# Weight conversion at the start of a fused FFT and MLP kernel: the clamps of fifteen weight blocks and six subtractions move from VectorE to GpSimd

## The chip, the cores and the metric

The kernel runs on one core of one Trainium2 chip. The metric is the device time of one execution in microseconds. Of the kernel before, three executions took 903.04, 904.01 and 903.05 us: a median of 903.05 us. The engines are named as the profile names them: PE (TensorE, the matmuls), DVE (VectorE), ACT (ScalarE), POOL (GpSimd) and SP (the queue that issues most DMAs).

## What is computed

A two-dimensional Fourier transform whose real part goes through an MLP with a gated activation:

```python
def _attn_ref(x):                       # x: 4 x 3008 x 256, float32
    X = np.fft.fft(x, axis=1)
    X = np.fft.fft(X, axis=2)
    return X.real.astype(np.float32)

def _moe_ref(x, w_in, w_out):           # 12032 x 256, 256 x 2048, 2048 x 256
    h = x @ w_in
    g = h * (1.0 / (1.0 + np.exp(-h)))
    return (g @ w_out).astype(np.float32)
```

`w_in` and `w_out` are float64. The chip has no such type here: the kernel reads each weight as two 32-bit words and builds the float32 out of their bits.

## The kernel before

The sequence transform is split into classes of output columns: 4 batches x 4 classes = 16 chunks `c` of 376 or 378 columns. The transform along the 256 features is folded into the weights: each of eight blocks of `w_in` (256 columns each) is multiplied by a DFT matrix (`project`, L523), and the products are kept in a high and a low part, `abh` and `abl` (`large` L532, `small` L536). A chunk then goes through 16 steps `f`, each of 128 hidden columns: `first` (L396 to L402) multiplies the chunk by `abh` and `abl` into the PSUM tile `pq` (two buffers), `act` (L414 to L431) adds and subtracts on DVE into `h` and takes the Silu on ACT into `g`, and `second` (L456 to L465), three steps behind, multiplies by `w_out` into four accumulators. In chunk 0 the first twelve steps use the whole float32 `w_out` block `wo_f32` (tile `wof`, L456); later steps use a high part `woh` and a low part `wol` (L458, L459, L465).

The order of instructions on each engine is the order in which this Python code emits them, and no scheduler changes it. Each engine runs its own list in order; semaphores tie the lists together. So an instruction that waits holds back all that stand behind it on its engine.

**The conversion of a block** is the generator `to_f32` (L70 to L85): an Abs on ACT (L77) of the upper word read as a float32, a clamp on DVE (L79), a double shift on DVE (L81), and two combined steps on DVE that bring in the lower word and the sign (L83, L85). Eight blocks of `w_in` (tile `wf`, raw tile `win`, four buffers) are converted between 4 and 40 us, each followed by `project`. In `ahead` (L512) a block's Abs is emitted; `convert` runs the rest. Eight blocks of `w_out` (raw tile `wo`, three buffers in two tags, so that block q + 3 is loaded when block q has been converted) follow from `convert_all_wo` (L124), a generator that yields between steps. The main loop draws on it: four `next` calls in step 0 of chunk 0, and in `act` two or three more per step (the argument `fill`), which places the steps between the additions of `h` on DVE. Blocks 0 to 5 become `wo_f32`; blocks 6 and 7 are split at once. Of blocks 0 to 5, `split_wo` (L116) makes the parts later: a copy to `woh` on ACT (L119) and a subtraction to `wol` on DVE (L121); these six lie between 71 and 108 us.

**GpSimd** issues some DMAs and does small arithmetic. In the first 110 us its list holds, in order: three fills, an accumulating DMA into the tile `raw` (`add_x`, L158) that waits for that tile's load, eight small DMAs of a row of the projected weights (L529) and one broadcast (`ub`, L377), five fills (L682, L288 to L290), a second `add_x` of 1 MB, three DMAs of the transform tables `te`, `to` and `t2` (L539, 1.1 MB each), and the subtractions `xl` of chunk 1's operand (L320). Ahead of its first arithmetic instruction the program has a row `ISA`, which loads the code that GpSimd needs for such arithmetic; fills and DMAs need none.

Of the kernel before, what the change touches and what calls it, by code (L numbers as in the profile page):

```python
# [24 lines left out]
F32 = mybir.dt.float32  # L25
# [4 lines left out]
ALU = mybir.AluOpType  # L30
# [15 lines left out]
W_MIN = float(np.uint32(896 << 20).view(np.float32))  # L46
W_MAX = float(np.uint32((1151 << 20) - 1).view(np.float32))
# [3 lines left out]
def fft_mlp(ctx, tc, x1, x2, w_in, w_out, te, to, t2, t2f, rot1, rot2, dft, eye, out):  # L51
    nc = tc.nc
    ctx.enter_context(tc.manual_schedule())
    tt = nc.vector.tensor_tensor
# [12 lines left out]
    zero = wts.tile([1, 256], F32, name="zero")  # L67
    turn = wts.tile([128, 1], F32, name="turn")
    vneg = fold_p.tile([128, 2, CH], F32R, tag="ri1", name="vneg")
    def to_f32(raw, dst):  # L70

        words = [raw.bitcast(d).rearrange("p c (n t) -> p c n t", t=2) for d in (U32, F32)]
        lo, hi, hf = words[0][:, :, :, 0], words[0][:, :, :, 1], words[1][:, :, :, 1]
        t = dst.bitcast(U32)
        nc.scalar.activation(dst, hf, AF.Abs)  # L77
        yield
        nc.vector.tensor_scalar(dst, dst, W_MIN, W_MAX, op0=ALU.max, op1=ALU.min)  # L79
        yield  # L80
        nc.vector.tensor_scalar(t, t, 5, 2, op0=ALU.logical_shift_left, op1=ALU.logical_shift_right)  # L81
        yield
        stt(t, lo, 29, t, op0=ALU.logical_shift_right, op1=ALU.bitwise_or)  # L83
        yield
        stt(t, hi, 0xC0000000, t, op0=ALU.bitwise_and, op1=ALU.bitwise_or)  # L85
# [13 lines left out]
    def load_wo(q, queue=nc.sync):  # L99

        tag = "od" if q % 3 == 2 else "ri0"
        wo_raw[q] = fold_p.tile([128, 2, D], I64, tag=tag, name="wo", bufs=1 + (tag == "ri0"))
        queue.dma_start(out=wo_raw[q], in_=w_out[q * 256:(q + 1) * 256, :].rearrange("(f p) d -> p f d", p=128))

    def convert_wo(q):
        if q < FULL // 2:
            yield from to_f32(wo_raw.pop(q), wo_f32[q])
            return
        wf = fold_p.tile([128, 2, D], F32, tag="half", name="wf", bufs=3)
        yield from to_f32(wo_raw.pop(q), wf)  # L110
        wh, wl = wo[0][q], wo[1][q]
        nc.scalar.activation(wh, wf, AF.Copy)
        yield
        tt(wl, wf, wh.bitcast(F32), op=ALU.subtract)

    def split_wo(q):  # L116
        wf, wh = wo_f32[q], wo[0][q]
        wl = wo[1][q] = wts.tile([128, 2, D], F32R, tag="wof", name="wol", bufs=FULL // 2 + 1)
        nc.scalar.activation(wh, wf, AF.Copy)  # L119
        yield 0.7  # L120
        tt(wl, wf, wh.bitcast(F32), op=ALU.subtract)  # L121
        yield 0.6

    def convert_all_wo():  # L124

        work = convert_wo(0)
        next(work)
        for q in range(NF // 2):
            for _ in range(2):
                next(work)  # L130
                yield
            if q + 1 < NF // 2:
                following = convert_wo(q + 1)
                next(following)
            yield from work
            if q + 3 < NF // 2:
                load_wo(q + 3)
            work = following
            yield
# [5 lines left out]
    def pq_tile():  # L145
        return pq_p.tile([128, 2, 512], F32, tag="pq", name="pq")
# [241 lines left out]
    def first(c, f):  # L388
        uvh, uvl, _, n, _ = chunks[c]
        fs = slice(f * 128, (f + 1) * 128)  # L390
        pq = pqs[c, f] = pq_tile()
        if c == 0 and f < DIRECT:
            for i, (vh, vl) in enumerate(((uvh[:, 1], uvl[:, 1]), (vneg[:, 0], vneg[:, 1]))):
                for m, (oh, ol) in enumerate(((uvh[:, 0], uvl[:, 0]), (vh, vl))):
                    for p, (a, x) in enumerate(((abh, oh), (abh, ol), (abl, oh))):
                        nc.tensor.matmul(pq[:, i, :n], a[:, m, fs], x[:, :n], start=m + p == 0, stop=m + p == 3)  # L396
            return
        for i in range(2):
            po = pq[:, i, :n]
            nc.tensor.matmul(po, abh[:, i, fs], uvh[:, i, :n], start=True, stop=False)  # L400
            nc.tensor.matmul(po, abh[:, i, fs], uvl[:, i, :n], start=False, stop=False)  # L401
            nc.tensor.matmul(po, abl[:, i, fs], uvh[:, i, :n], start=False, stop=True)  # L402
    def signs(c, f):

        return (slice(0, 1), slice(1, 2)) if c == 4 * B - 1 and f >= NF - 2 else (slice(0, 2),)

    def act(c, f, fill=()):
        pq, (_, _, ub, n, _) = pqs.pop((c, f)), chunks[c]
        direct = c == 0 and f < DIRECT
        if not direct:  # L410
            h = mp.tile([128, 2, CH], F32, tag="h", name="h", bufs=3)
            p = h[:, 1]
        if not direct:
            stt(p[:, :n], ub[:, :n], a128[f // 2][:, f % 2:f % 2 + 1], pq[:, 0, :n], op0=ALU.mult, op1=ALU.add)  # L414
        for work in fill[:1]:
            next(work, None)
        if not direct:
            tt(h[:, 0, :n], p[:, :n], pq[:, 1, :n], op=ALU.add)  # L418
            tt(h[:, 1, :n], p[:, :n], pq[:, 1, :n], op=ALU.subtract)  # L419
        for work in fill[1:]:  # L420
            next(work, None)
        if c == 0 and f < FULL:
            g = gp.tile([128, 2, CH], F32, tag=("gh", "gl")[f % 2], name="g")
            nc.scalar.activation(g[:, :, :n], (pq if direct else h)[:, :, :n], AF.Silu)
            gs[c, f] = g
            return
        gh = gp.tile([128, 2, CH], F32R, tag="gh", name="gh")
        gl = gp.tile([128, 2, CH], F32R, tag="gl", name="gl")
        for sg in signs(c, f):
            nc.scalar.activation(h[:, sg, :n], h[:, sg, :n], AF.Silu)  # L430
            nc.scalar.activation(gh[:, sg, :n], h[:, sg, :n], AF.Copy)  # L431
        gs[c, f] = gh, gl, h
# [73 lines left out]
    win, wf32, pws, conv = {}, {}, {}, {}  # L506
# [4 lines left out]

    def ahead(q):  # L512
        wf32[q] = fold_p.tile([128, 2, 256], F32, tag="half", name="wf", bufs=3)
        conv[q] = to_f32(win.pop(q), wf32[q])
        next(conv[q])

    def project(q):

        w = wf32.pop(q)
        pw = pws[q] = ps.tile([128, 2, 256], F32, tag="ps", name="pw")  # L520
        for m in range(2):
            for c in range(2):
                nc.tensor.matmul(pw[:, m, :256], dft_sb[:, c, m, :], w[:, c], start=c == 0, stop=c == 1)  # L523
# [10 lines left out]
    def small(q):  # L534
        fs = slice(q * 256, (q + 1) * 256)
        tt(abl[:, :, fs], pws.pop(q)[:, :, :256], abh[:, :, fs].bitcast(F32), op=ALU.subtract)  # L536
# [70 lines left out]
    wo_work = convert_all_wo()  # L607
# [28 lines left out]
    for b in range(1, B - 1):  # L636
        c = 4 * b + 1
# [10 lines left out]
    for n in range(len(steps) + LAG):  # L648
        c, f = steps[min(n, len(steps) - 1)]
        if n < len(steps):  # L650
            first(c, f)
        if n == 0:
            project(7)
            for _ in range(4):
                next(wo_work)
            small(6)
        if n >= LAG:
            second(*steps[n - LAG])
        new = None
        if n < len(steps):  # L660
            if f == 12 and c + 1 < 4 * B:
                drain(queue, upto=("op", c + 1))
                drain(pool_queue, upto=("x", c + 1))
                new = pq_tile()
                transform(c + 1, new)
            act(c, f, (2 + (1 < f < 12)) * (wo_work,) if c == 0 else ())
        if n == 0:
            large(7)
            small(7)
            late.close()  # L670
            acc_p = ctx.enter_context(tc.tile_pool(name="acc", bufs=1, space=PSUM))
            tabs_p = ctx.enter_context(tc.tile_pool(name="tabs", bufs=1))
        if n == 4:
            add_x(0, 0)
            for name, t in (("te", te), ("to", to)):
                tabs[name] = tabs_p.tile([128, 2, 3, 376], F32R, name=name)
                load_tables(name, t)
            tabs["t2"] = wts.tile([128, 2, 3, 376], F32R, tag="t2", name="t2")
            load_tables("t2", t2)
        if c == 0 and f == DIRECT:  # L680
            for a in (abh, abl):
                nc.gpsimd.memset(a[0:1, 1, :DIRECT * 128].bitcast(F32), 0.0)  # L682
        if 1 <= n <= len(steps):
            rest(*steps[n - 1])
        if new:
            spread(c + 1, new)
        if n < len(steps):
            for fn, a in plan.get((c, f), ()):
                fn(*a)
            drain(queue, 0.6)  # L690
            drain(pool_queue, 1.3 if c == 1 else 0.6)
# [106 lines left out]
```

## Time and profile before

| what | value |
|---|---|
| median of three executions | 903.05 us (903.04 to 904.01) |
| profiled execution, first to last instruction | 901.8 us |
| TensorE busy, share of the span | 881.9 us, 98% |
| VectorE busy | 743.9 us, 82% |
| ScalarE busy | 525.8 us, 58% |
| GpSimd busy | 179.4 us, 20% |
| mean granted TensorE clock, share of full speed | 0.997 |

The profiled execution is one more execution of the same program. Its own total is not listed apart from its span; the span lies 1.25 us under the median of the three. A row of the profile's timeline gives the start and the length of an instruction, and in brackets how long the engine stood idle before it and who ended that. Length includes the time until the result is written, so two instructions that follow each other may overlap by about 0.1 us. A row of the table by stretches gives the busy time of each engine, the granted clock as a share of 2.4 GHz, and what the DMA engines moved. "Wait" rows say which engine stood idle, and which instruction of another engine ended that.

### The profile page before, as it was taken

To read this page: it belongs to the slowest core of one execution; us is meant where nothing else is said; L and a number is where in the kernel's file an instruction comes from. 1 tells how busy PE (TensorE), PEld (TensorE's weight loads), DVE (VectorE), ACT (ScalarE), POOL (GpSimd) and SP (SyncE) were. 2 spreads that over 40 slices of the span, in tenths; PEclk is the share of its full clock that TensorE was granted. 3 is DMA by queue.
4 is the path that set the end of the run, shared out by engine and by line. 5 is a ranking of instruction groups with operands and counts; after the bars stand their busy time and mean duration, and the time that the engine had idled before them with its cause. 6 is when DMAs were issued, how large, how long until landed. Compare 5 with 4: busy or idle time off the path is not lost.

```text
span 901.8 us, 12782 instructions
## 1 busy us (share of the span) xinstructions
PE 881.9 (98%) x4982; PEld 858.9 (95%) x4982; DVE 743.9 (82%) x1209; ACT 525.8 (58%) x728; POOL 179.4 (20%) x213
## 2 busy tenths in 40 slices
PE   6889999999999999999999999999999999999998
PEld 4567999999999999999999999999999999999998
DVE  6888888978889797987879698887879878786885
ACT  3625675646667564755746475665645656565554
POOL 1114051660123061460301025110100101010000
PEclk9999999999999999999999999999999999999999
DMA  9790315312030460203021060212103021210301
GB/s 297 159 300 8 44 24 79 82 5 39 1 29 17 71 159 4 41 1 25 20 10 35 3 134 1 10 35 9 35 2 42 1 9 35 9 35 1 44 1 35
DMA packets 19597, 42.65 MB, mean 47 GB/s; under 512 B 2464, under 2 KB 12704, under 8 KB 17616
## 3 DMA queue, kind: packets, MB, share of 16 engines
q1 hardware_dynamic: 17904, 31.87, 18.9%
q0 software_dynamic: 1632, 9.96, 5.5%
q8 instruction: 39, 0.64, 0.3%
q14 instruction: 22, 0.18, 0.1%
HBM read 26.39 MB, written 12.34 MB: 43 GB/s over the span
## 4 chain that ended last, share of the span: by engine, by line
PE 92%; DVE 4%; DMA 2%; issue 1%; ACT 1%; SPq 0%; DVEq 0%; ACTq 0%
PE acc L459 19%; PE acc L465 19%; PE acc L458 19%; PE pq L400 9%; PE pq L401 9%; PE pq L402 9%; PE pq L345 5%; DMA wo<-in_w_out_dram 1%; DMA win<-in_w_in_dram 1%; PE acc L456 1%; PE pq L210 1%; DVE wf L83 1%; PE pw L523 0%; DVE wf L85 0%; DVE wf L79 0%
## 5 line engine op out<-in xcount | busy, mean ns | idle before, releaser
L430 ACT ACTIVATE h<-h 128x752 f32<-128x752 f32 (+2 forms) x246 | 204.0, 829 | 284.3 <-DVE h L419 281.7
L459 PE MATMUL acc<-gh,wol 128*128 128x376 f32 (+1 forms) x976 | 326.8, 335 | 0.0
L458 PE MATMUL acc<-gh,woh 128*128 128x376 f32 (+1 forms) x976 | 326.3, 334 | 0.0
L441 DVE TENSOR_TENSOR gl<-h,gh 128x752 fp32r<-128x752 f32 (+2 forms) x246 | 242.0, 984 | 1.9 <-ACT gh L431 1.8
L465 PE MATMUL acc<-gl,woh 128*128 128x376 f32 (+1 forms) x976 | 216.1, 335 | 0.0
L431 ACT ACTIVATE gh<-h 128x752 fp32r<-128x752 f32 (+2 forms) x246 | 204.2, 830 | 7.8
L414 DVE SCALAR_TENSOR_TENSOR h<-ub,a,pq 128x376 f32<-128x376 f32 (+1 forms) x254 | 153.5, 604 | 58.3 <-PE pq L402 56.2
L459 PEld LDWEIGHTS acc<-gh,wol 128*128 128x128 f32 x976 | 183.7, 188 | 0.0
L458 PEld LDWEIGHTS acc<-gh,woh 128*128 128x128 f32 x976 | 183.5, 188 | 0.0
L400 PE MATMUL pq<-uvh,abh 128*128 128x376 f32 (+1 forms) x508 | 173.7, 342 | 2.8 <-DVE h L419 2.8
L465 PEld LDWEIGHTS acc<-gl,woh 128*128 128x128 f32 x976 | 172.8, 189 | 0.0
L401 PE MATMUL pq<-uvl,abh 128*128 128x376 f32 (+1 forms) x508 | 170.4, 335 | 0.0
L402 PE MATMUL pq<-uvh,abl 128*128 128x376 f32 (+1 forms) x508 | 170.2, 335 | 0.0
L419 DVE TENSOR_TENSOR h<-h,pq 128x376 f32<-128x376 f32 (+1 forms) x254 | 139.0, 547 | 8.7
L418 DVE TENSOR_TENSOR h<-h,pq 128x376 f32<-128x376 f32 (+1 forms) x254 | 138.9, 547 | 8.5
L320 POOL TENSOR_TENSOR xl<-xf,xh 128x256 fp32r<-128x256 f32 x53 | 49.6, 964 | 399.6 <-DVE h L419 244.6
L400 PEld LDWEIGHTS pq<-uvh,abh 128*128 128x128 f32 x508 | 95.6, 188 | 5.3 <-DVE h L419 4.0
L401 PEld LDWEIGHTS pq<-uvl,abh 128*128 128x128 f32 x508 | 95.9, 189 | 1.1
L402 PEld LDWEIGHTS pq<-uvh,abl 128*128 128x128 f32 x508 | 96.0, 189 | 0.0
L378 DVE TENSOR_TENSOR uvl<-pq,uvh 128x752 fp32r<-128x752 f32 (+1 forms) x16 | 15.1, 943 | 56.1 <-ACT row L376 56.1
L259 POOL TENSOR_TENSOR ri<-ri,raw 128x256 f32<-128x256 f32 (+1 forms) x28 | 27.5, 994 | 106.6 <-ACT ri L255 106.3
L456 PE MATMUL acc<-g,wof 128*128 128x376 f32 x96 | 33.5, 492 | 0.0
(117 smaller groups left out, 515.2 us busy)
## 6 DMA issues: line engine op xcount, KB each, us to landing
out_dram<-o SPq DMA_DIRECT2D x48, 188.0 KB, 2.3
raw<-in_x_dram SPq DMA_DIRECT2D x5, 1024.0 KB, 11.1
raw<-in_x_dram POOLq DMA_DIRECT2D x5, 1024.0 KB, 8.5
win<-in_w_in_dram SPq DMA_DIRECT2D x8, 512.0 KB, 9.4
wo<-in_w_out_dram SPq DMA_DIRECT2D x8, 512.0 KB, 9.9
out_dram<-o SPq DMA_DIRECT2D x16, 189.0 KB, 2.4
ub<-row SPq DMA_DIRECT2D x11, 188.0 KB, 8.7
te<-in_te_dram POOLq DMA_DIRECT2D x1, 1128.0 KB, 13.2
```

The lines of the kernel that those rows point to most:

```text
L400: nc.tensor.matmul(po, abh[:, i, fs], uvh[:, i, :n], start=True, stop=False)
L401: nc.tensor.matmul(po, abh[:, i, fs], uvl[:, i, :n], start=False, stop=False)
L402: nc.tensor.matmul(po, abl[:, i, fs], uvh[:, i, :n], start=False, stop=True)
L414: stt(p[:, :n], ub[:, :n], a128[f // 2][:, f % 2:f % 2 + 1], pq[:, 0, :n], op0=ALU.mult, op1=ALU.add)
L418: tt(h[:, 0, :n], p[:, :n], pq[:, 1, :n], op=ALU.add)
L419: tt(h[:, 1, :n], p[:, :n], pq[:, 1, :n], op=ALU.subtract)
L430: nc.scalar.activation(h[:, sg, :n], h[:, sg, :n], AF.Silu)
L431: nc.scalar.activation(gh[:, sg, :n], h[:, sg, :n], AF.Copy)
L441: tt(gl[:, sg, :n], g[:, sg, :n], gh[:, sg, :n].bitcast(F32), op=ALU.subtract)
L458: nc.tensor.matmul(po, wo[0][f // 2][:, f % 2, es], gh[:, sg, :n], start=f == 0, stop=False)
L459: nc.tensor.matmul(po, wo[1][f // 2][:, f % 2, es], gh[:, sg, :n], start=False, stop=False)
L465: nc.tensor.matmul(accs[c][i][:, :n], wo[0][f // 2][:, f % 2, es], gl[:, sg, :n], start=False, stop=f == NF - 1)
```

## The change

The clamp of every block but block 0 of `w_in` is issued on GpSimd. With it the place of a yield changes: for these blocks the clamp is emitted right behind the Abs, in one step of the generator, so a block of `w_out` has one step less. Accordingly `convert_all_wo` draws one step instead of two ahead of the next block's Abs, the main loop draws three instead of four in step 0, and `act` two in every step. The subtraction of `split_wo` goes to GpSimd too, with a budget of 0.1 instead of 0.6 in the queue that spreads VectorE's extra work.

```diff
-    def to_f32(raw, dst):
+    def to_f32(raw, dst, engine=nc.gpsimd):
...
         nc.scalar.activation(dst, hf, AF.Abs)
-        yield
-        nc.vector.tensor_scalar(dst, dst, W_MIN, W_MAX, op0=ALU.max, op1=ALU.min)
-        yield
+        if engine is nc.vector:
+            yield
+        engine.tensor_scalar(dst, dst, W_MIN, W_MAX, op0=ALU.max, op1=ALU.min)
+        if engine is not nc.vector:
+            yield
         nc.vector.tensor_scalar(t, t, 5, 2, op0=ALU.logical_shift_left, op1=ALU.logical_shift_right)
...
-        tt(wl, wf, wh.bitcast(F32), op=ALU.subtract)
-        yield 0.6
+        nc.gpsimd.tensor_tensor(wl, wf, wh.bitcast(F32), op=ALU.subtract)
+        yield 0.1
...
         for q in range(NF // 2):
-            for _ in range(2):
-                next(work)
-                yield
+            next(work)
+            yield
...
-        conv[q] = to_f32(win.pop(q), wf32[q])
+        conv[q] = to_f32(win.pop(q), wf32[q], nc.gpsimd if q else nc.vector)
...
-            for _ in range(4):
+            for _ in range(3):
                 next(wo_work)
...
-            act(c, f, (2 + (1 < f < 12)) * (wo_work,) if c == 0 else ())
+            act(c, f, 2 * (wo_work,) if c == 0 else ())
```

Lines below the top of `to_f32` shift by one to three in the changed file (L79 becomes L80, L81 L83, L83 L85, L85 L87, L121 L123, L158 L159, L320 L321, L424 L425).

The order at three places, before and now. The first is GpSimd's list at the start of the program, from the fill of `turn` on (`raw_128` is the tile that is accumulated into; `wf_170`, `wf_182`, `wf_208` are blocks 1, 2 and 3 of `w_in`; `a128` are the small DMAs). Before:

```order
L559 MEMSET turn_86 1x1
L158 DMA raw_128<-in_x2_dram 64x2048
L529 DMA a128_0_77<-rows_121 128x1x2
L529 DMA a128_1_78<-rows_121 128x1x2
L529 DMA a128_2_79<-rows_121 128x1x2
```

Now:

```order
L560 MEMSET turn_86 1x1
L159 DMA raw_128<-in_x2_dram 64x2048
L80 ISA
L80 TENSOR_SCALAR wf_170<-wf_170 128x512
L80 TENSOR_SCALAR wf_182<-wf_182 128x512
L530 DMA a128_0_77<-rows_121 128x1x2
L530 DMA a128_1_78<-rows_121 128x1x2
L80 TENSOR_SCALAR wf_208<-wf_208 128x512
L530 DMA a128_2_79<-rows_121 128x1x2
```

The code load and the clamps of blocks 1 and 2 stand behind the first accumulating DMA, and each later clamp between the small DMAs.

The second is ScalarE's list where the steps of chunk 0 begin (`wof_99`, `wof_100`, `wof_101` are blocks 3, 4 and 5 of `w_out`; `g` are the Silus of f = 0 to 3, `pq_372` and `pq_376` the PSUM tile of f = 1). Before:

```order
L424 ACTIVATE g_357<-pq_328 128x2x376
L528 ACTIVATE rows_121<-pw_341 1x256
L531 ACTIVATE pw_341<-zero_85 1x256
L532 ACTIVATE abh_75<-pw_341 128x2x256
L424 ACTIVATE g_389<-pq_372 128x2x376
L77 ACTIVATE wof_99<-wo_350 128x512
L424 ACTIVATE g_408<-h_398 128x2x376
```

Now:

```order
L425 ACTIVATE g_361<-pq_329 128x2x376
L529 ACTIVATE rows_121<-pw_342 1x256
L532 ACTIVATE pw_342<-zero_85 1x256
L533 ACTIVATE abh_75<-pw_342 128x2x256
L77 ACTIVATE wof_99<-wo_351 128x512
L425 ACTIVATE g_393<-pq_376 128x2x376
L425 ACTIVATE g_410<-h_402 128x2x376
```

The Abs of block 3, which waits for that block's load, has moved ahead of the Silu of f = 1.

The third is GpSimd's list around the second accumulating DMA and the tables. Before:

```order
L290 MEMSET xf_437 64x2x129
L158 DMA raw_132<-in_x1_dram 128x2048
L539 DMA te_467<-in_te_dram 128x2256
L539 DMA to_469<-in_to_dram 128x2256
L539 DMA t2_471<-in_t2_dram 128x2256
L320 ISA
```

Now:

```order
L80 TENSOR_SCALAR wof_100<-wof_100 128x512
L289 MEMSET xf_441 128x2x128
L290 MEMSET xf_441 64x2x127
L291 MEMSET xf_441 64x2x129
L80 TENSOR_SCALAR wof_101<-wof_101 128x512
L159 DMA raw_132<-in_x1_dram 128x2048
L540 DMA te_470<-in_te_dram 128x2256
L540 DMA to_472<-in_to_dram 128x2256
L540 DMA t2_474<-in_t2_dram 128x2256
```

These four DMAs stand behind the clamps of blocks 0 to 5 of `w_out`, the last two of which are shown.

## Rows read from the trace of the kernel before

**Rows 1.** The page: the span's busy times by engine, and TensorE in 40 slices.
```profile
PE 881.9 (98%) x4982; PEld 858.9 (95%) x4982; DVE 743.9 (82%) x1209; ACT 525.8 (58%) x728; POOL 179.4 (20%) x213
...
PE   6889999999999999999999999999999999999998
```

**Rows 2.** Busy us (instructions) of each engine by stretch, granted clock, DMA share, GB/s.
```profile
14.50:25.20 10.70, 10.59 (x32) 6.00 (x32) 7.66 (x10) 2.85 (x7) 1.10 (x2) 1.00 1.05 336
...
25.20:39.00 13.80, 9.38 (x37) 6.61 (x37) 12.68 (x27) 9.13 (x20) 2.21 (x4) 1.00 0.79 163
...
100.00:500.00 400.00, 400.00 (x2326) 400.00 (x2326) 340.93 (x545) 251.12 (x351) 120.26 (x134) 1.00 0.22 38
```

**Rows 3.** TensorE's waits from 0 to 100 us: total us, times, longest.
```profile
PE pw L523 <- DVE wf L85: 10.5, 4, 7.8
PE pq L400 <- DVE h L419: 2.8, 2, 2.5
```

**Rows 4.** Timeline of TensorE: start, us, instruction, count, idle before and its end.
```profile
7.82 6.05 PE L523 MATMUL pw<-wf,dft_sb 128*128 128x256 f32 x16 [7.82 <-DVE wf L85]
14.54 1.99 PE L523 MATMUL pw<-wf,dft_sb 128*128 128x256 f32 x8 [0.67 <-DVE wf L85]
...
34.27 1.97 PE L523 MATMUL pw<-wf,dft_sb 128*128 128x256 f32 x8 [0.83 <-DVE wf L85]
37.37 1.97 PE L523 MATMUL pw<-wf,dft_sb 128*128 128x256 f32 x8 [1.14 <-DVE wf L85]
...
66.61 0.44 PE L400 MATMUL pq<-uvh,abh 128*128 128x376 f32 x1 [2.49 <-DVE h L419]
...
86.48 0.87 PE L345 MATMUL pq<-te,xh 128*128 128x190 f32 x4
```

**Rows 5.** Timeline of GpSimd.
```profile
10.41 0.95 POOL L158 DMA_DIRECT2D raw<-in_x_dram  x1 [9.17 <-DMA raw<-in_x_dram]
...
46.63 0.90 POOL L158 DMA_DIRECT2D raw<-in_x_dram  x1
...
70.60 5.30 POOL L320 TENSOR_TENSOR xl<-xf,xh 128x256 fp32r<-128x256 f32 x5 [21.43 <-ACT xh L313]
```

**Rows 6.** Timeline of VectorE.
```profile
12.14 0.43 DVE L79 TENSOR_SCALAR wf<-wf 128x512 f32<-128x512 f32 x1 [2.19 <-ACT wf L77]
12.61 0.43 DVE L81 TENSOR_SCALAR wf<-wf 128x512 uint32<-128x512 uint32 x1
13.07 0.69 DVE L83 SCALAR_TENSOR_TENSOR wf<-win,wf 128x512 uint32<-128x512 uint32 x1
13.79 0.69 DVE L85 SCALAR_TENSOR_TENSOR wf<-win,wf 128x512 uint32<-128x512 uint32 x1
...
42.11 0.69 DVE L85 SCALAR_TENSOR_TENSOR wof<-wo,wof 128x512 uint32<-128x512 uint32 x1
...
78.02 1.13 DVE L83 SCALAR_TENSOR_TENSOR wf<-wo,wf 128x512 uint32<-128x512 uint32 x1
```

**Rows 7.** GpSimd by line and shape, whole span: busy us, mean ns, idle before.
```profile
L182 POOL TENSOR_TENSOR sm<-raw 128x258 f32<-128x258 f32 x8 | 6.0, 747 | 0.6
...
L228 POOL TENSOR_TENSOR raw<-raw 128x512 f32<-128x512 f32 x2 | 2.6, 1298 | 0.0
```

**Rows 8.** DMA issues at 42.5 to 45 and 49 to 51 us: KB, us to landing.
```profile
wo<-in_w_out_dram SPq DMA_DIRECT2D x1, 512.0 KB, 3.5
...
wo<-in_w_out_dram SPq DMA_DIRECT2D x1, 512.0 KB, 12.8
```

**Rows 9.** Timeline of ScalarE: the Silu of f = 1, Abs of w_out blocks 3 and 5.
```profile
45.22 0.80 ACT L424 ACTIVATE g<-pq 128x752 f32<-128x752 f32 x1 [0.64 <-PE pq L396]
46.44 0.68 ACT L77 ACTIVATE wof<-wo 128x512 f32<-128x512 f32 x1 [0.41 <-DMA wo<-in_w_out_dram]
...
62.52 0.66 ACT L77 ACTIVATE wof<-wo 128x512 f32<-128x512 f32 x1 [5.72 <-DMA wo<-in_w_out_dram]
```

**Rows 10.** Busy us and granted clock after the hole at 64 us, columns as in rows 2.
```profile
67.20:70.60 3.40, 3.40 (x9) 2.31 (x8) 3.06 (x7) 2.64 (x4) 0.00 (x1) 0.50 0.23 85
```

## The prediction

> **What bounds the kernel now.** I read the busy times first. TensorE is busy for 881.9 of 901.8 us, VectorE for 82% of the span [rows 1]. The table by stretches says where the rest lies: between 100 and 500 us TensorE is busy in all 400 us; from 25.2 to 39 us it is busy in 9.38 of 13.80, and VectorE there in 12.68 [rows 2]. So a change to the weights' conversion can only earn or lose in the first 100 us. The list of TensorE's waits in that stretch names 10.5 us for converted weights (7.8 of it before the first matmul) and 2.8 us for `h` [rows 3]. The timeline puts them in place: 0.83 us before block 5, 1.14 us before block 6, 2.49 us at 64 us [rows 4]. After that hole the granted clock is at the lower of its two levels, 1.2 GHz, from 67.20 to 70.60 us [rows 10].
>
> The profiled execution spans 901.8 us; the median of the three runs is 903.05 us, 1.25 us more, which lies around the span. I add a shift to the median, since the change touches nothing there.
>
> **Part 1, the start.** The sixteen matmul rows of blocks 0 and 1 run from 7.82 us without a break; block 2 is converted at 14.48 us (13.79 + 0.69) and its eight matmuls end at 14.54 + 1.99 = 16.53 us [rows 4, 6]. From block 2 to 25.2 us TensorE is busy in 10.59 of 10.70 us [rows 2], so what delays block 2 delays everything. In the changed order GpSimd's clamp of block 1 stands behind the accumulating DMA, which starts at 10.41 us because it waits 9.17 us for its tile, and holds GpSimd until 11.36 us [rows 5]. Between the two stands the `ISA` row that loads the code for GpSimd's arithmetic. Today it stands ahead of the first subtraction at 70.60 us, in an idle stretch of 21.43 us [rows 5], so no row shows its length: it is bounded by 0 and 21.4 us. I take it for a transfer from memory, so the nearest row is a transfer alone on the queues: w_out block 3 lands 3.5 us after its issue [rows 8]. I take 3.5 us. The clamp itself has no row either. A fill or copy in half the time is excluded by nothing, so below stands 0.4 us, the 0.43 us of VectorE's own kind of instruction [rows 6]; above stands the two-input 128x512 instruction, 1298 ns; nearest is the 128x258 sum, which reads as many values as the clamp, 747 ns [rows 7]. I take 0.75 us.
>
> So block 1 is clamped at 11.36 + 3.5 + 0.75 = 15.6 us, and VectorE's other three steps take 14.48 - 12.61 = 1.87 us [rows 6]: 17.5 us. TensorE has then been idle since about 11 us. Its first sixteen matmuls, from rest, took 6.05 us, 0.38 each, where block 2's eight took 1.99, 0.25 each [rows 4]; after a hole of some 6 us I expect that first pace again: blocks 1 and 2 end at 17.5 + 6.05 = 23.5 us, **7.0 us late**. With no load and no slower pace, VectorE's blocks 1 and 2 end at 11.36 + 0.75 + 2 x 1.87 = 15.85 us, 1.4 us late: that is the low end. Block 3's clamp waits for two small DMAs on GpSimd but is needed only 3.4 us after block 2, beside other matmuls: nothing. GpSimd's other DMAs (eight small ones and `ub`) move behind clamps, and land several us before their readers: nothing while these leads last.
>
> The Trainium skill, GPSIMD Engine Reference, section Instruction dispatch, says that the first call after such a load pays some 6 us that no row shows; no run here shows it. By its figure part 1 would be an estimated 9.5 us and the sum 2.5 us higher.
>
> **Part 2, blocks 4 to 6.** Three clamps leave VectorE ahead of block 6, worth 12.61 - 12.14 = 0.47 us each if nothing takes their place, so up to 1.4 of the 1.97 us of holes [rows 4, 6]. But while GpSimd works, VectorE's instructions stretch: at 78.02 us the line that takes 0.69 us alone took 1.13 us [rows 6]. A clamp of the next block now runs beside each block's steps, and 0.44 us lost cancels 0.47 gained. I take 0, with -1.4 and +0.3 as ends.
>
> The Trainium skill, SBUF — State Buffer, section SBUF: two separate sides, speaks against the change here: GpSimd and a VectorE instruction with two SBUF inputs exclude each other for a whole instruction, where I count a stretch. The trace agrees in kind, since 1.13 us is 0.44 over 0.69. By a full exclusion each clamp would cost what it saves and more, and the sum would be an estimated 1 us higher.
>
> **Part 3, a new wait on ScalarE.** The order shows the Abs of w_out block 3 moved ahead of the Silu of f = 1. That Silu ended at 45.22 + 0.80 = 46.0 us today, and block 3's Abs began at 46.44 us [rows 9], 3.5 us after the load, whose issue had to wait for VectorE to finish block 0 at 42.80 us (42.11 + 0.69) [rows 6, 8]. Now the Silu ends at 46.44 + 0.68 + 0.80 = 47.9 us plus the shift, and TensorE, which needs that PSUM tile back for f = 3, waits **1.9 us**. VectorE lost two more clamps before block 0 is done, so 0.9 us is the low end; two more stretches of 0.44 us make 2.8 us the high end, and a hole that long could bring the lower clock again: 1.7 us (half of the 3.40 us at 0.50 [rows 10]).
>
> **Part 4, the hole at 64 us.** Today GpSimd issues 1 MB of accumulation and three tables at 46.63 us, and w_out blocks 5 and 6 share the DMA engines with them: 12.8 us to land instead of 3.5 [rows 5, 8]. ScalarE stands at block 5's Abs for 5.72 us until 62.52 us [rows 9], and TensorE waits 2.49 us. In the changed order those four DMAs stand behind the clamp of block 5, hence behind its load, and block 6's load is issued before them too. This frees the 2.8 us of waits for `h` [rows 3] and 1.7 us of the lower clock: **-4.5 us**. Late next is block 7, which now meets the tables; its Abs stands before the Silu of f = 7, wanted three steps of 3.5 us later. That cover holds by about 2 us; if it is gone, 2.5 us come back. The tables themselves are first read at 86.48 us [rows 4], 20 us after they land: nothing.
>
> **Part 5, six subtractions.** On VectorE they take 0.69 us each, on GpSimd 1.30 us [rows 7]. They lie between 71 and 110 us, where TensorE has no hole but the one counted, and their results are read from 98 us on. Nothing, unless GpSimd is several us behind there.
>
> **Sum:** 7.0 + 0 + 1.9 - 4.5 = +4.4 us, so 903.05 + 4.4 = **907.5 us**.
>
> **The rivals.**
> 1. *The load of GpSimd's code is not felt* (the code is resident, or comes in a few hundred ns). For it: no row shows a load, and the first subtraction at 70.60 us starts without any visible delay. Against it: that row had 21 us of cover. Then part 1 is 1.4, part 2 -0.7, part 3 0.9, part 4 -4.5: -2.9 us, **900.1 us**. It decides below a load of 1.1 us.
> 2. *No load, but the hole still costs pace and the engines disturb each other.* Block 1 at 13.98 us, sixteen matmuls in 6.05 us: 20.0 us, 3.5 late. 3.5 + 0 + 1.9 - 4.5 = +0.9 us, **904.0 us**.
> 3. *The load takes as long as a transfer under traffic*, 12.8 us [rows 8], or the whole idle stretch: part 1 is 9.3 to 17.9 us longer, **917 to 925 us**.
>
> That the change does not do what it says is excluded by the order.
>
> **Chances and range.** The forecast with loads between 1.5 and 8 us: 0.47. Rival 1: 0.33, since nothing in the trace excludes it. Rival 2: 0.13. Rival 3: 0.07. This kernel's measurement tells changes over 0.2%, 1.8 us: faster 0.33, same 0.13, slower 0.54. The low end is rival 1 with part 2 at its full -1.4: -3.6, so 899.5 us. The high end is a load of 8 us, 4.5 over mine, with part 3 at its 2.8 us and part of the lower clock: some +10.5 us, 913.5 us. The forecast's own range is 905 to 913.5 us.
>
> **What would show it.** In the profile after: an idle stretch on GpSimd between its DMA at 10.4 us and the first clamp (3 us and more, or none); TensorE's block 2 ending near 23.5 us, or near 18; no hole before blocks 5 and 6 that is larger than now; ScalarE's Abs of w_out block 3 waiting for its DMA ahead of a Silu, with a hole on TensorE before f = 3; `wo` loads of some 4 us for blocks 5 and 6, and no hole at f = 7. A first clamp at 11.4 us would prove the forecast wrong, and so would a hole at f = 7 that stays.

## The result, and the profile after

The changed kernel took **910.63 us** (median of five executions, 908.95 to 911.57), the kernel before 903.46 us (five on the same chip, 903.04 to 904.08): a ratio of **1.0073, with a 95% interval of 1.0061 to 1.0085**. It is slower, by 7.2 us; forecast were 907.5 us, in a range of 899.5 to 913.5. The profiled execution took 911.57 us, its span is 909.8 us. Of `e1_win_vector` and `e8_sub_only`, further down, one execution each took over 2000 us; the ratios leave it out, and since that one is the profiled one of `e8_sub_only`, no trace of this kernel is read. Line numbers from the clamp on are one or two higher than before (the clamp is L80, the next steps L83 to L87, the Silu L425).

The page's rows that answer to [rows 1], and the list of TensorE's waits from 0 to 110 us, as in [rows 3]:

```profile
PE 885.0 (97%) x4982; PEld 860.6 (95%) x4982; DVE 738.4 (81%) x1188; ACT 525.6 (58%) x728; POOL 216.0 (24%) x234
...
PE   4889999999999999999999999999999999999998
```
```profile
PE pw L524 <- DVE wf L87: 15.2, 5, 7.8
PE pq L401 <- ACT g L425: 2.8, 1, 2.8
PE pq L335 <- DVE xf L273: 2.5, 1, 2.5
```

VectorE was relieved of 5.5 us, GpSimd took on 36.6 us (216.0 - 179.4). TensorE waits 15.2 us for converted weights where it waited 10.5, and a wait of 2.8 us for ScalarE's Silu has taken the place of the 2.8 us for `h`. The first slice of the 40 fell from 6 tenths to 4. Where the waits are shows in TensorE's timeline, which answers to [rows 4]:

```profile
7.84 3.54 PE L524 MATMUL pw<-wf,dft_sb 128*128 128x256 f32 x8 [7.84 <-DVE wf L87]
16.63 5.99 PE L524 MATMUL pw<-wf,dft_sb 128*128 128x256 f32 x16 [5.25 <-DVE wf L87]
...
26.39 1.99 PE L524 MATMUL pw<-wf,dft_sb 128*128 128x256 f32 x8 [0.34 <-DVE wf L87]
...
34.35 5.75 PE L335 MATMUL pq<-t2f,xf 128*128 128x376 f32 x12 [2.53 <-DVE xf L273]
...
44.20 1.97 PE L524 MATMUL pw<-wf,dft_sb 128*128 128x256 f32 x8 [0.64 <-DVE wf L87]
...
49.36 1.99 PE L524 MATMUL pw<-wf,dft_sb 128*128 128x256 f32 x8 [1.13 <-DVE wf L87]
...
57.29 0.44 PE L401 MATMUL pq<-uvh,abh 128*128 128x376 f32 x1 [2.84 <-ACT g L425]
...
58.42 4.39 PE L457 MATMUL acc<-g,wof 128*128 128x376 f32 x8
...
94.37 0.87 PE L346 MATMUL pq<-te,xh 128*128 128x190 f32 x4
```

From the two timelines comes the ledger of the change, by where TensorE begins a stage:

| TensorE | before, us | after, us | late by | what was added |
|---|---|---|---|---|
| block 2's matmuls end | 16.53 | 22.62 | 6.1 | hole of 5.25 before block 1, slow matmuls after it |
| f = 0 begins | 38.99 | 45.81 | 6.8 | 0.34 before block 3, 1.7 lower clock in the transform, less 1.3 of holes |
| f = 1 begins | 42.77 | 51.00 | 8.2 | 1.13 before block 7 |
| f = 3 begins | 46.08 | 57.29 | 11.2 | 2.84 for the Silu of f = 1 |
| f = 4 begins | 49.45 | 62.36 | 12.9 | lower clock: eight matmuls in 4.39, not 2.69 us |
| second transform begins | 86.48 | 94.37 | 7.9 | the hole at 64 us and the lower clock after it are gone: -5.0 |

From there to the end nothing more is lost or won (the spans differ by 8.0 us). The 1.7 us in the transform belong to this execution: in six other traces the same matmuls after the same wait stay at full clock (last section). GpSimd's timeline, against [rows 5], and its groups by line for the first 110 us, against [rows 7]:

```profile
10.84 0.97 POOL L159 DMA_DIRECT2D raw<-in_x_dram  x1 [9.61 <-DMA raw<-in_x_dram]
11.68 4.09 POOL L80 TENSOR_SCALAR wf<-wf 128x512 f32<-128x512 f32 x2
...
63.46 1.92 POOL L80 TENSOR_SCALAR wof<-wof 128x512 f32<-128x512 f32 x1
65.33 0.92 POOL L159 DMA_DIRECT2D raw<-in_x_dram  x1
```
```profile
L80 POOL TENSOR_SCALAR wf<-wf 128x512 f32<-128x512 f32 x9 | 17.5, 1981 | 18.5 <-ACT wf L77 18.4
L80 POOL TENSOR_SCALAR wof<-wof 128x512 f32<-128x512 f32 x6 | 12.0, 2003 | 3.6 <-ACT wof L77 3.4
L123 POOL TENSOR_TENSOR wol<-wof,woh 128x512 fp32r<-128x512 f32 x5 | 6.9, 1374 | 14.6 <-ACT woh L121 8.9 <-issue 5.7
```

The first clamp starts at 11.68 us, right behind the DMA: there is **no idle stretch for a load of code**. The record of that load (`MODIFY_POOL_CONFIG`) is at 11.6 us and lasts 0.29 us, inside the DMA's row. But a clamp takes 1.9 to 2.0 us on GpSimd, against 0.43 us on VectorE [rows 6], and more than the subtraction, which reads two inputs. VectorE's first step on block 1 starts at 13.93 us and takes 1.19 us, where the same step on block 2 took 0.43 us in the kernel before [rows 6]:

```profile
13.93 1.19 DVE L83 TENSOR_SCALAR wf<-wf 128x512 uint32<-128x512 uint32 x1 [6.22 <-POOL wf L80]
```

The table by stretches shows what the hole does to the clock (columns as in [rows 2]); ScalarE's timeline shows the new wait, as [rows 9] showed the old order; and the row of the DMA issues between 57 and 63 us answers to [rows 8]:

```profile
11.40:16.60 5.20, 0.00 (x0) 0.00 (x0) 2.60 (x4) 1.41 (x3) 4.95 (x4) 0.79 1.04 353
16.60:22.60 6.00, 5.97 (x17) 4.92 (x18) 2.98 (x5) 1.91 (x4) 0.63 (x2) 0.61 1.02 339
...
58.80:62.20 3.40, 3.40 (x7) 1.89 (x6) 3.37 (x8) 1.92 (x3) 2.02 (x3) 0.50 0.48 154
```
```profile
55.88 0.68 ACT L77 ACTIVATE wof<-wo 128x512 f32<-128x512 f32 x1 [3.08 <-DMA wo<-in_w_out_dram]
56.45 0.79 ACT L425 ACTIVATE g<-pq 128x752 f32<-128x752 f32 x1
```
```profile
wo<-in_w_out_dram SPq DMA_DIRECT2D x2, 512.0 KB, 3.7
```

The Abs of `w_out` block 3 stands for 3.08 us and the Silu of f = 1 behind it. The `w_out` loads that took 12.8 us [rows 8] now take 3.7 us, since the tables are issued at 65.3 us and later.

### The profile page after: what moved, and what is told of

It reads as the page before. It is cut to its first block, busy times and chain, and to the rows that moved or that the text cites. A ratio compares the mean times of both kernels' runs of the same rounds, so it can differ in the third digit from the quotient of the medians.

```text
span 909.8 us, 12798 instructions
## 1 busy us (share of the span) xinstructions
PE 885.0 (97%) x4982; PEld 860.6 (95%) x4982; DVE 738.4 (81%) x1188; ACT 525.6 (58%) x728; POOL 216.0 (24%) x234
## 4 chain that ended last, share of the span: by engine, by line
PE 95%; ACT 1%; DMA 1%; DVE 1%; POOL 1%; issue 0%; SPq 0%; POOLq 0%
PE acc L460 19%; PE acc L466 19%; PE acc L459 19%; PE pq L401 10%; PE pq L402 10%; PE pq L403 10%; PE pq L346 5%; PE acc L457 4%; DMA raw<-in_x_dram 1%; PE pw L524 1%; PE pq L335 1%; POOL wf L80 0%; DMA wo<-in_w_out_dram 0%; PE pq L211 0%; ACT wof L77 0%
## 5 line engine op out<-in xcount | busy, mean ns | idle before, releaser
L321 POOL TENSOR_TENSOR xl<-xf,xh 128x256 fp32r<-128x256 f32 x53 | 48.5, 941 | 380.9 <-DVE h L420 194.3
## 6 DMA issues: line engine op xcount, KB each, us to landing
te<-in_te_dram POOLq DMA_DIRECT2D x1, 1128.0 KB, 11.4
```

## The experiments

Twelve kernels ran, each beside the kernel before on the same chip; a ratio is to that one. On record were: the start is the loss (the clamp's price and its place in GpSimd's list); a load of GpSimd's code is the loss; the `w_out` part is the loss; and, for what came back, the tables' DMAs against VectorE's relief.

### The start

**`w_in` clamps back on VectorE** (`e1_win_vector`):

```diff
-        conv[q] = to_f32(win.pop(q), wf32[q], nc.gpsimd if q else nc.vector)
+        conv[q] = to_f32(win.pop(q), wf32[q], nc.vector)
```

> The changed kernel with the clamps of all eight w_in blocks back on VectorE; the w_out clamps and the six subtractions stay on GpSimd. Head theory (the loss lies in block 1's chain, where the clamp takes 1.91 us instead of 0.42 and stands behind the accumulating DMA): the first step of f = 0 starts near 39 us again instead of 45.8, the hole of some 2.8 us at f = 3 stays and may bring the lower clock for 3.4 us, the hole at f = 7 stays away; the time is 901 to 904 us, 7 to 9 us under the changed kernel. Rival (the loss comes from the w_out blocks on GpSimd and from VectorE's steps stretching beside GpSimd): at most 2 us under the changed kernel, 908 us or more.

Measured: 903.51 us, ratio 1.0 (0.9991 to 1.001). f = 0 begins at 39.4 us and the hole before f = 3 is there, 3.19 us:

```profile
49.84 0.44 PE L401 MATMUL pq<-uvh,abh 128*128 128x376 f32 x1 [3.19 <-ACT g L425]
```

So the whole loss goes with the seven clamps of `w_in`; with a quick start the rest of the change, wait and gain together, is worth nothing.

**Only those seven on GpSimd** (`e2_win_gpsimd`), in the kernel before:

```diff
-    def to_f32(raw, dst):
+    def to_f32(raw, dst, engine=nc.vector):
...
-        yield
-        nc.vector.tensor_scalar(dst, dst, W_MIN, W_MAX, op0=ALU.max, op1=ALU.min)
+        if engine is nc.vector:
+            yield
+        engine.tensor_scalar(dst, dst, W_MIN, W_MAX, op0=ALU.max, op1=ALU.min)
         yield
...
-        conv[q] = to_f32(win.pop(q), wf32[q])
+        conv[q] = to_f32(win.pop(q), wf32[q], nc.gpsimd if q else nc.vector)
```

> The kernel before with nothing changed but the clamps of w_in blocks 1 to 7, which run on GpSimd. Head theory: TensorE waits some 5 us before block 1, f = 0 starts near 45.8 us (6.8 later), the tables' DMAs still meet w_out blocks 5 and 6 and the hole at f = 7 stays, so the time is the changed kernel's and the 4.5 us that it got back there: 910 to 915 us. Rival (the w_out part is the cost): 903 to 906 us.

Measured: 912.88 us, ratio 1.0102 (1.0089 to 1.0116). TensorE waits 4.99 us before block 1, and after 60 us there are holes of 2.22, 0.58, 2.00 and 0.94 us:

```profile
16.57 6.31 PE L524 MATMUL pw<-wf,dft_sb 128*128 128x256 f32 x16 [4.99 <-DVE wf L86]
```

Both experiments say that the start is the loss, 7 to 9 us of it; the `w_out` part, worth nothing with a quick start, gives back some 2 us behind a late one (912.88 against 910.63).

**The accumulating DMA behind block 1's clamp** (`e4_add_behind`), in the changed kernel:

```diff
-    add_x(1, 0, lo)
...
     ahead(1)
+    add_x(1, 0, lo)
     convert(0)
```

> The changed kernel with one DMA moved: the first accumulating DMA on GpSimd stands behind the clamp of w_in block 1 instead of ahead of it. Place theory (two thirds of the loss in the head is the wait behind that DMA): block 1's clamp starts near 6.7 us, TensorE's hole before block 1 goes, one of some 2 us remains before block 2, f = 0 starts 3 to 4.5 us earlier than in the changed kernel, and the time is 905.5 to 908 us. Rival 1 (the 1.9 us of each clamp and the lower clock are the loss, wherever the first stands): 908.5 to 911 us. Rival 2 (loading GpSimd's code takes several us which the wait for the DMA had covered): the clamp starts at 8 us or later, and the time lies between.

Measured: 906.41 us, ratio 1.0031 (1.0019 to 1.0042), some 4 us under the changed kernel. GpSimd's and TensorE's timelines:

```profile
7.47 1.92 POOL L80 TENSOR_SCALAR wf<-wf 128x512 f32<-128x512 f32 x1 [6.24 <-ACT wf L77]
11.48 1.03 POOL L159 DMA_DIRECT2D raw<-in_x_dram  x1 [2.09 <-DMA raw<-in_x_dram]
13.05 1.92 POOL L80 TENSOR_SCALAR wf<-wf 128x512 f32<-128x512 f32 x1 [0.54 <-ACT wf L77]
```
```profile
8.27 5.39 PE L524 MATMUL pw<-wf,dft_sb 128*128 128x256 f32 x16 [8.27 <-DMA dft_sb<-in_dft_dram]
16.93 1.99 PE L524 MATMUL pw<-wf,dft_sb 128*128 128x256 f32 x8 [3.28 <-DVE wf L87]
```

The place theory holds: the clamp starts as soon as ScalarE's Abs is done, and blocks 0 and 1 run without a break again. What is left is a hole of 3.28 us before block 2 (I had expected 2 us), and no lower clock follows it. Block 2's clamp stands behind the DMA in GpSimd's list, but what it waits for last is its own Abs on ScalarE, which waited for the block's load until 12.27 us. Block 2's matmuls end at 18.92 us (16.93 + 1.99), 3.7 us earlier than in the changed kernel. The same run shows the middle blocks at full clock: holes of 0.47, 0.52 and 0.67 us before blocks 4, 5 and 6, and 1.14 before block 7.

**One operation instead of two** (`e6_one_op`). It leaves out the upper bound of every clamp.

```diff
-        engine.tensor_scalar(dst, dst, W_MIN, W_MAX, op0=ALU.max, op1=ALU.min)
+        engine.tensor_scalar(dst, dst, W_MIN, None, op0=ALU.max)
```

> The changed kernel with GpSimd's clamps cut to the lower bound alone (the upper bound is left out, on VectorE's block 0 too): one arithmetic operation per value in place of two. Theory of passes (GpSimd's 1.91 us is two operations per value one after the other): each clamp takes some 0.95 to 1.1 us; block 1 is ready 0.9 us earlier, the hole before block 2's weights shrinks likewise and the holes before blocks 3, 6 and 7 close or shrink, 906.5 to 909 us. Rival (the form of the instruction sets the time, whatever the number of operations): 1.8 to 1.95 us each and 910 to 911 us.

Measured: 909.14 us, ratio 1.0066 (1.0053 to 1.0079). The groups by line on GpSimd:

```profile
L80 POOL TENSOR_SCALAR wf<-wf 128x512 f32<-128x512 f32 x9 | 13.9, 1588 | 18.6 <-ACT wf L77 18.6
L80 POOL TENSOR_SCALAR wof<-wof 128x512 f32<-128x512 f32 x6 | 9.4, 1570 | 5.6 <-ACT wof L77 5.6
```

Neither theory's number: the clamp falls by 0.4 us, not by half and not by nothing. A part of it is paid per operation, but most of the time stays with one.

### The tables' DMAs

**Only those four late** (`e3_tables_late`), in the kernel before:

```diff
+    late_t = wts.tile([1, 1], F32, name="late_t")
...
-        if n == 4:
+        if n == 6:
+            nc.gpsimd.tensor_copy(late_t, wo_f32[4][0:1, 0, 0:1])
             add_x(0, 0)
```

> The kernel before with every clamp and subtraction on VectorE; the second accumulating DMA and the three table DMAs are issued at step 6 instead of 4, behind a copy of one value of the converted w_out block 4 on GpSimd, so that the loads of w_out blocks 5 to 7 are issued first. Theory (the changed kernel's gain after 60 us comes from those four DMAs being late alone, not from VectorE's relief): loads of 3.5 to 4 us for blocks 5 and 6, no hole of 2.5 us at f = 7 and no lower clock after it, 898 to 900 us (4 to 5 us under before). Rival (VectorE's queue, with fewer clamps, is what closed that hole): 902 to 904 us, the hole there in some form.

Measured: 901.6 us, ratio 0.9975 (0.9966 to 0.9984): 2.2 us under before, not 4 to 5. The DMA issues from 49.5 to 61 us, and TensorE's timeline; then the same two transforms in the kernel before:

```profile
wo<-in_w_out_dram SPq DMA_DIRECT2D x3, 512.0 KB, 3.9
```
```profile
72.41 0.44 PE L401 MATMUL pq<-uvh,abh 128*128 128x376 f32 x1 [0.85 <-DVE h L420]
...
83.00 0.88 PE L346 MATMUL pq<-te,xh 128*128 128x190 f32 x4
...
826.99 2.23 PE L346 MATMUL pq<-to,xh 128*128 128x376 f32 x12
```
```profile
829.22 2.23 PE L345 MATMUL pq<-to,xh 128*128 128x376 f32 x12
```

The mechanism is shown: with every clamp on VectorE the hole at 64 us and the lower clock after it go when the four DMAs are late, and the second transform begins 3.5 us earlier than at 86.48 us [rows 4]. A hole of 0.85 us came at f = 10. The other miss was new to me: between those two transforms TensorE never waits in either kernel, yet this one takes 743.99 us where before takes 742.74, so 1.25 us of the gain are given back.

**With the subtractions on GpSimd too** (`e10_no_clamps`), on top of that:

```diff
         yield 0.7
-        tt(wl, wf, wh.bitcast(F32), op=ALU.subtract)
-        yield 0.6
+        nc.gpsimd.tensor_tensor(wl, wf, wh.bitcast(F32), op=ALU.subtract)
+        yield 0.1
```

> The kernel before with all clamps on VectorE, the tables' DMAs behind the conversion of w_out block 4 as in the run named e3_tables_late, and the six subtractions of the split on GpSimd. Theory (what is left in that run, a hole of 0.85 us at f = 9, is VectorE's queue, stretched beside GpSimd and holding one of the subtractions for 1.21 us): the hole goes, 900 to 901 us, 0.5 to 1.5 under that run. Rival (GpSimd's later sums become late, or the stretch takes what the move saves): 901.5 us or more.

Measured: 901.07 us, ratio 0.9976 (0.9966 to 0.9986). The hole at f = 10 fell to 0.28 us as expected, but the time did not follow: it is 2.2 us under the kernel before on the same chip, as the run without this edit was (ratio 0.9975). The medians, 901.07 and 901.6 us, are of two chips. It shows the slower pace as well (743.99 us from 82.54 to 826.53 us).

**The six subtractions alone** (`e8_sub_only`), in the kernel before:

```diff
-        tt(wl, wf, wh.bitcast(F32), op=ALU.subtract)
-        yield 0.6
+        nc.gpsimd.tensor_tensor(wl, wf, wh.bitcast(F32), op=ALU.subtract)
+        yield 0.1
```

> The kernel before with the six subtractions of the split on GpSimd and all clamps on VectorE. Theory (they lie where TensorE has no hole that depends on them): within 1 us of the kernel before, 902.5 to 904.5 us. Rival 1 (VectorE relieved of 6 times 0.7 to 1.2 us closes part of the hole near 64 us or the small ones after it): 900 to 902 us. Rival 2 (GpSimd becomes late for the next operand): over 905 us.

Measured: 902.42 us, ratio 0.9985 (0.9974 to 0.9996). That is 0.1 us under the interval that I gave for no effect; rival 2 is out, between the other two it doesn't decide, and without a trace it stays open where such a gain would lie.

### ScalarE's order

**Abs of block 3 behind the Silu of f = 1** (`e5_abs_later`), in the changed kernel:

```diff
-            act(c, f, 2 * (wo_work,) if c == 0 else ())
+            act(c, f, (2 - (f == 1)) * (wo_work,) if c == 0 else ())
...
-        if n == 4:
+        if n == 5:
             add_x(0, 0)
```

> The changed kernel with one step of the w_out conversion drawn less at f = 1, so that the Abs of w_out block 3 stands behind the Silu of f = 1 again as in the kernel before (the tables' DMAs are issued at step 5 instead of 4, so that they stay behind block 5's clamp). Theory (the wait of 2.8 us before f = 3 and the 1.7 us of lower clock after it come from that place alone): no hole before f = 3, 906 to 907.5 us, 3 to 4.5 under the changed kernel. Rival (the block is only late next: the same wait appears at f = 4 or later, because every w_out block is late): 909 to 911 us.

Measured: 910.56 us, ratio 1.0084 (1.0069 to 1.0099): the theory's 3 to 4.5 us did not come. The hole before f = 3 is gone, but the wait came back far behind it. ScalarE's and TensorE's timelines:

```profile
82.27 0.67 ACT L77 ACTIVATE wf<-wo 128x512 f32<-128x512 f32 x1 [6.17 <-DMA wo<-in_w_out_dram]
```
```profile
85.28 0.45 PE L401 MATMUL pq<-uvh,abh 128*128 128x376 f32 x1 [1.89 <-DVE h L420]
```

One step less at f = 1 makes all later blocks one step later. Block 7's load is issued between the tables, lands 13 us later, and the Silus behind its Abs are late for f = 11.

**The same with the `w_in` clamps on VectorE** (`e7_both`), in the changed kernel:

```diff
-        conv[q] = to_f32(win.pop(q), wf32[q], nc.gpsimd if q else nc.vector)
+        conv[q] = to_f32(win.pop(q), wf32[q], nc.vector)
...
-            act(c, f, 2 * (wo_work,) if c == 0 else ())
+            act(c, f, (2 - (f == 1)) * (wo_work,) if c == 0 else ())
...
-        if n == 4:
+        if n == 5:
```

> The w_in clamps on VectorE as in the first experiment, the w_out clamps and the six subtractions on GpSimd, and the Abs of w_out block 3 behind the Silu of f = 1 as in the experiment beside this one. If the first experiment's remaining loss was the wait of 3.2 us before f = 3 and the 1 us of lower clock after it, the time is 899 to 900.5 us, 3.5 to 4.5 under the kernel before. Rival (another wait takes its place within the next steps): 901.5 to 904 us.

Measured: 903.87 us, ratio 1.0004 (0.9993 to 1.0015). The rival again, and with the lower clock:

```profile
77.89 0.45 PE L401 MATMUL pq<-uvh,abh 128*128 128x376 f32 x1 [2.26 <-DVE h L420]
79.05 4.38 PE L457 MATMUL acc<-g,wof 128*128 128x376 f32 x8
```

**And the tables one step later still** (`e9_three`), on top of that:

```diff
-        if n == 5:
+        if n == 6:
             add_x(0, 0)
```

> The kernel of the run named e7_both (w_in clamps on VectorE, Abs of w_out block 3 behind the Silu of f = 1) with the second accumulating DMA and the three table DMAs one step later, behind the clamp of w_out block 6, so that the load of block 7 is issued ahead of them. Theory (in that run the wait only moved on to block 7, whose load met the tables and took 13.8 us; TensorE stood 2.3 us before f = 10 and ran at the lower clock after it): block 7 lands in 4 to 6 us, no hole between f = 3 and f = 12 over 1 us, 899.5 to 901 us. Rival (the tables are then late for the second transform at about 84 us, or block 7 is not what f = 10 waited for): 903 us or more.

(The text counts the step one short: the hole was before f = 11.) Measured: **899.94 us, ratio 0.9967 (0.9955 to 0.9979)**, the fastest kernel here with the run below, 3.3 us under before and about 10 us under the changed kernel. Block 7's load, and all waits of TensorE from 0 to 110 us:

```profile
wo<-in_w_out_dram SPq DMA_DIRECT2D x1, 512.0 KB, 3.6
```
```profile
PE pw L524 <- DVE wf L87: 10.1, 4, 7.6
PE pq L335 <- DVE xf L273: 2.5, 1, 2.5
PE acc L457 <- DVE abl L537: 0.5, 1, 0.5
PE pq L401 <- DVE h L420: 0.3, 1, 0.3
```

So the wait on ScalarE, once removed alone, comes back at block 7, and both edits together free both. The tables' edit without the other was not run on this kernel.

**Blocks 4 to 6 alone on GpSimd** (`e11_mid_gpsimd`), on top of that:

```diff
-        conv[q] = to_f32(win.pop(q), wf32[q], nc.vector)
+        conv[q] = to_f32(win.pop(q), wf32[q], nc.gpsimd if 4 <= q <= 6 else nc.vector)
```

> The kernel of the run beside this one named e9_three with the clamps of w_in blocks 4 to 6 on GpSimd. It asks for the price of those three alone, off the start. Theory of my prediction (0, between -1.4 and +0.3 us): the holes before blocks 4 to 7 add up to between 0.6 and 2.3 us (1.97 before). Rival (each clamp's 1.91 us against 0.43 is felt, as in the run named e4_add_behind, where the four holes add up to 2.8 us): 0.8 us or more above e9_three.

Measured: 900.1 us, ratio 0.9965 (0.9953 to 0.9978). No difference: these three cost nothing and bring nothing.

**The two edits in the changed kernel** (`e12_after_mended`), `w_in` clamps on GpSimd as there:

```diff
-            act(c, f, 2 * (wo_work,) if c == 0 else ())
+            act(c, f, (2 - (f == 1)) * (wo_work,) if c == 0 else ())
...
-        if n == 4:
+        if n == 6:
```

> The changed kernel, w_in clamps on GpSimd included, with the two edits of the run named e9_three: Abs of w_out block 3 behind the Silu of f = 1, tables' DMAs behind the clamp of w_out block 6. Only the start differs from that run. Theory (the wait of part 3 is worth 2.8 us and, where it comes, 1.7 us of lower clock, once it is not handed on to block 7; the start costs 6 to 8 us): 906 to 908 us, 3 to 4.5 under the changed kernel and 6 to 8 over e9_three. Rival (with all blocks late by the start's delay the wait comes back elsewhere): 909 us or more.

Measured: 907.95 us, ratio 1.0045 (1.0032 to 1.0059). Against the changed kernel's 1.0073 that is 0.28%, 2.5 us: the price of the new wait, less than the 3 to 4.5 that I expected (in the two profiled executions, both with the lower clock in the first transform, the second transform begins 3.4 us apart, at 94.37 and 90.95 us). Against 0.9967 for the same kernel with `w_in` on VectorE it is 0.78%, **7.0 us: the price of the start**.

## Why the prediction was right, and where it was not

The sign, the range and the places were right, and the forecast was 3 us low. But the reason given for its largest term was wrong, by the prediction's own sign: a first clamp at 11.4 us was to prove it wrong, and the first clamp starts at 11.68 us, right behind the DMA. With the load at nothing and the rest as it stood, the sum is rival 2's, 904.0 us, 6.6 us under the measured time. That the forecast came as near as it did is luck: terms that were too small or missing (the clamp, VectorE's first step, block 7, part 3) stood in for the load.

- **Part 1, the start: +7.0 forecast, +6.1 to block 2's end.** Three terms failed and nearly cancelled. *The load of GpSimd's code*, taken at 3.5 us, is not felt: rival 1's condition held, and yet the kernel is slower, because *the clamp*, taken at 0.75 us between 0.4 and 1.30, takes 1.91 us at the least, and *VectorE's first step* beside the next clamp takes 1.19 us instead of 0.43. My bound rested on the two-input subtraction as the dearest kind of row; it wasn't a bound for another operation. From the clamp's start at 11.68 us to VectorE's at 13.93 and the end of its three steps, block 1 was ready at 16.6 us, not 17.5. That step was stretched and not shut out: it ended at 15.12 us, ahead of the clamp beside it (15.77 us by the profile). The Trainium skill, GPSIMD Engine Reference, section Instruction dispatch, lets the first call behind a load pay some 6 us; here the clamp starts 0.84 us after the DMA does and 0.1 us after the load's record, so the trace disagrees for this code. What is not shown is whether the transfer begins at its record or ahead of it, while GpSimd waited for 9.61 us. The record was in the trace of the kernel before as well, at 49.1 us and 0.05 us long, 21 us ahead of the first subtraction; the prediction had looked at the idle stretch alone.
- **The sixteen matmuls after the hole** took 5.99 us, as I took from the first sixteen of the program (6.05 us [rows 4]). The granted clock is 0.61 in that stretch and fell during the hole. Whether the first sixteen ran at the lower level too isn't shown: the trace of the kernel before has its first clock record at about 12.6 us, when most of them were done. So the pace was right, and its cause is known for the second case alone.
- **"Block 3's clamp ... nothing", and block 7, which had no term:** holes of 0.34 and 1.13 us. Block 7's chain from its Abs to its last step takes 5.2 us (44.11 to 49.30 us), where it took 3.25 us before (36.82 to 40.07 us), and TensorE comes to wait for it. So the longer chain is felt wherever TensorE catches up with a block, not at the first alone. Block 7's cost is 1.4 us in the ledger.
- **Part 2, blocks 4 to 6: 0 forecast.** Shown by the run that has these three alone on GpSimd (900.1 against 899.94 us): there, one block's clamp runs beside the steps of the block ahead of it. In the run with full clock there the three holes add up to 1.66 us against 1.97 before.
- **Part 3, the Silu of f = 1: 1.9 forecast, 2.84 and 1.7 of lower clock found**, the forecast's high end. Mechanism and place were right; undone together with its consequence at block 7 it is worth 2.5 us by the medians.
- **Part 4, the hole at 64 us: -4.5 forecast, -5.0 in the ledger.** The hole stands before f = 8, which the prediction counted as f = 7. A hole costs more than its bracket says, since it also breaks the overlap of matmuls that follow each other: from the start of a group of `acc` matmuls (2.69 us long) to the next `pq` it is 2.24 us without a hole (57.88 to 60.12 us) and 5.18 us with this one of 2.49 us (61.43 to 66.61 us). That is about the 0.5 us between forecast and ledger. That it is the DMAs' place and not VectorE's relief is shown by the run that moves them alone. The forecast's "cover of about 2 us" for block 7 held in the changed kernel; one step less at f = 1 used it up.
- **Part 5, the subtractions: 0 forecast,** between 0 and 1.4 us of gain by the ratios of the two runs that move them.

Rows against the sum: 6.1 + 0.7 + 1.4 + 3.0 + 1.7 - 5.0 = 7.9 us at the second transform, where the forecast had 4.4. The 3.5 us between them: the start 0.9 less, block 3 and the first transform's clock 0.7 more, block 7 1.4 more, part 3 2.8 more, part 4 0.5 better.

## What to carry to other kernels

Price a moved instruction on its new engine by a row of the same operation there; where none exists, leave the upper bound open instead of closing it with another kind of instruction. Moving work off a busy engine helps only where that engine is what the path waits for; here the chain Abs, clamp, three steps is serial for each block, so an engine that takes 1.5 us longer lengthens it however idle it is. When one wait is removed, look for the next load or step that was behind it in the same queue, and move both before judging the edit.

## What the runs showed of the hardware

- GpSimd's `tensor_scalar` with two operations on 128x512 float32 values took 1.91 us when nothing disturbed it, 1.48 us with one operation, while a two-input `tensor_tensor` of that shape took 1.28 to 1.30 us; VectorE does the two-operation clamp in 0.42 us. The Trainium skill, GPSIMD Engine Reference, section Engine selection, calls one-input work on GpSimd roughly line-rate; this trace doesn't bear that out, by a factor of 4.5 against VectorE.
- The same wait brings the lower clock in one execution and not in another. After a wait of 2.5 us before the first transform the granted clock fell in seven of thirteen profiled executions (0.66 to 0.75 over the next 5 us), and the twelve matmuls took 5.5 to 5.75 us; it stayed at 1.00 in six, where they took 4.06 us. These are thirteen kernels with one execution each, so they do not tell the execution from the kernel. The kernel before does: of its 68 executions with a recorded mean clock, nine stayed at 1.000 and took 902.15 us (median), the other 59 took 903.62 us. So some 1.5 us of a single run's time hang on this, a part of this kernel's spread (901.0 to 905.2 us over the chips used). The length of a hole alone does not decide: those of 3.6 to 5.3 us at the start were followed by the lower level all five times, the one of 3.28 us was not, and the one of 2.49 us at 64 us was.
- The two kernels with the four-byte tile `late_t` ran 0.17% slower with no wait on TensorE anywhere: 743.99 us in both from the second to the last transform, where the eleven other profiled kernels took 742.74 to 742.76 us. The tile shifts what is allocated behind it; whether that is the cause, or the copy into it, wasn't tried.
